# Chunk 0 of a Fourier mixing and gated feed-forward kernel: the E part added on TensorE, output-weight forms in pairs, weight pieces in another order

## The chip, the cores and the metric

The kernel runs on one core of one Trainium2 chip. The metric is the device time of one execution in microseconds (us). Engines are called TensorE (PE; PEld is its weight load), VectorE (DVE), ScalarE (ACT), GpSimd (POOL) and SyncE (SP, which here only issues DMA transfers).

## The reference

```python
x: (8, 3008, 256)                     # batch, sequence S, features D
X = fft(x, axis=1); X = fft(X, axis=2)
y = X.real.reshape(24064, 256)
gate = 1 / (1 + exp(-(y @ w_gate)))   # w_gate, w_val: (256, 1536)
val  = y @ w_val
out  = (gate * val) @ w_out           # w_out: (1536, 256)
```

All of it is float32 in the reference. The weights may arrive as 64-bit floats; the kernel then turns them into 32-bit ones itself.

## The kernel before, in words

The transform over the features is folded into the weights: `merge` (matmuls `ps`) multiplies pieces of `w_gate` and `w_val` by a 256-wide table `dt`, which gives G1 and G2. The transform over the sequence is done by matmuls with cosine and sine tables (`st`, matmuls `ev` and `od`), which give for each of the eight inputs a row set P (`pk`) and a row set Q (`qk`) over the frequencies. One extra row E (tile `ek`, for input 0) belongs to the middle feature. Frequency k and its mirror share the work: the pre-activation at one of them is G1·P + ge·E + G2·Q, at the other G1·P + ge·E − G2·Q.

**The main loop** runs over steps i: eight inputs, six chunks of 252 frequencies each, twelve steps for the twelve blocks of 128 hidden units. Chunk 0 of input 0 is steps 0 to 11. A step issues, in this order:

- `front_a(i)`: matmuls `pf<-pk,G` (G1·P), for gate and value, into a bank `PF[i]`. From step 12 on, ScalarE has put ge·E into the bank before (`seed`, L506).
- `part(i)`: `AP[i]` (tile `ae`), which keeps G1·P + ge·E before G2·Q comes in. Steps 0 to 11: two VectorE instructions L523. Later steps: one ScalarE instruction (L520) that doubles.
- `gate_a(i-1)` and `gate_b(i-1)`: the sigmoid on ScalarE (L539), the mirror's pre-activations z = 2·(G1·P + ge·E) − PF on VectorE (L541, or L544 where ScalarE doubled), gate times value (L556), the mirror's sigmoid on ScalarE (L557), its product on VectorE (L558), and the sums `sf` of H blocks on POOL (L562: seven in one step of three, six in the next).
- weights: what `pre`, `use` and `parts_` hold for the step (below).
- `back`: from step 5, ten matmuls `po` with a third of the 15 products of a group of three hidden blocks; they use `wf`, sums of quarter blocks of the output weights.
- `front_b(i)`: matmuls `pf<-qk,G` (G2·Q) into the same bank.

Before step 0 the row E is copied into the first 252 columns of row 0 of `qk` (L694), so that in chunk 0 these matmuls add ge·E to the bank themselves.

**Weights.** They come in 18 pieces (`jobs`: w is 0 gate, 1 value, 2 output; c counts 256 columns or rows). `weight_load` issues the DMA. `weight_parts` (two ScalarE instructions, L261 and L262) and `weight_join` (three on VectorE, L271, L272 and L274, then one on POOL, L276) turn a piece of 64-bit floats into 32-bit ones. `weight_use` runs `merge` on a gate or value piece (matmuls `ps`, then two ScalarE copies into G2 and G1, L297 and L298, and transfers `ge<-G` of row 0 of G2, L300), or, for an output piece, enters `forms(g)`: per group g of three blocks, 4 scaled copies on ScalarE (L315) and 11 sums or differences (L317), on POOL for g < 2 and on VectorE for g = 2, 3, in two parts of 6 and 5. One part is taken up per step. Pieces 0 to 8 are joined before step 0, piece 9 in step 0, pieces 10 to 17 in steps 1 to 8. Pieces from 10 on share three raw slots: the load of piece j+3 waits until POOL has joined piece j.

**Queues.** Every engine runs its instructions in the order in which the program issues them. The SP queue also waits, before each DMA, for the transfer eight lanes earlier. Before the loop, VectorE alternates between joining pieces and putting the sums of the transform in place (`then`, L420 and L423).

Of the kernel before, what the change touches and what calls it, by code (L numbers as in the profile page):

```python
# [48 lines left out]
NQ = 6  # L49
# [5 lines left out]
              (15, 4, 6, 1)),  # L55
          2: ((11, 8, 11, 0), (12, 8, 12, 0), (9, 5, 9, 0), (10, 10, 5, 0), (16, 2, 11, 0),
              (16, 9, 16, 0))}
W_SUMS = ((1, 5, 1), (3, 5, 1), (7, 2, 0), (6, 0, 0), (0, 7, 1), (4, 9, 0), (4, 8, 0), (3, 6, 1),
          (2, 3, 0), (2, 6, 1), (0, 1, 0))
W_COPIES = ((2, -1), (0, 1), (4, 1), (5, 1))  # L60

PRODUCTS = ((0, 12), (1, 11), (4, 9), (6, 4), (2, 13), (5, 5), (13, 0), (8, 6), (11, 2), (12, 8), (9, 3),
            (10, 10), (14, 1), (15, 7), (16, 14))
PLACE = (0, 1, 2, 5, 3, 4, 6, 7, 8, 9, 10, 11, 14, 13, 12)


# [11 lines left out]
def kernel(  # L78
# [108 lines left out]

    def load_table(t, nq):
        for q in range(0, NQ, nq):
            nc.sync.dma_start(out=ST[0][0:NP, t, q : q + nq], in_=stab[:, t, q : q + nq])  # L190

    def mirror_tables():
        return mirrored(tr, stab, NE)
# [7 lines left out]

    jobs = [(w, c - (w == 2)) for c in range(NPR + 1) for w in range(3)
            if (c if w == 2 else c < NPR)]
    RAW, WS = {}, {}
    shared = {}
    KEEP = 10
# [1 line left out]
    def weight_load(j):  # L210


        w, c = jobs[j]
        src = (moe_w_gate, moe_w_val, moe_w_out)[w]
        src = src[2 * c * P : 2 * (c + 1) * P, :] if w == 2 else src[:, c * WC : (c + 1) * WC]
        src = src.rearrange("(c p) f -> p c f", p=P)

        def some(n, pool, tag):

            if tag not in shared:  # L220
                shared[tag] = pool.tile([P, n * WC], F32, name=f"w{tag}", tag=tag)
            return shared[tag]

        def home(j):

            if j in (0, 1, 2, 3, 5):
                if j > 2:
                    ws = some(4, pqp, "qk")[:, (j // 5) * 2 * WC : (j // 5 + 1) * 2 * WC]
                    return sp.tile([P, 4 * WC], F32, name="raw", tag="sf"), ws
                t = hp.tile([P, 6 * WC], F32, name="raw", tag="h")  # L230
                return t[:, 0 : 4 * WC], t[:, 4 * WC :]
            if j in (4, 6, 9):
                t = wf[:, {4: 1, 6: 2, 9: 3}[j]].rearrange("p m n -> p (m n)")
                return t[:, 0 : 4 * WC], t[:, 4 * WC : 6 * WC]
            t = some(10, cp, "c")
            if j == 7:
                raw = pqp.tile([P, 4 * WC], F32, name="raw", tag="pk")
                return raw, t[:, 6 * WC : 8 * WC]
            return t[:, 0 : 4 * WC], t[:, 4 * WC : 6 * WC]

        if j < KEEP:
            raw, ws = home(j)
        else:
            both = some(24, xp, "x4").rearrange("p (i n) -> p i n", n=2 * WC)
            r, i = (j - KEEP) % 3 * 2, 6 + (j - KEEP) % 6
            raw, ws = both[:, r : r + 2].rearrange("p a n -> p (a n)"), both[:, i]
        raw = raw.bitcast(I32).rearrange("p (c f w) -> p c f w", c=2, w=2)
        ws = ws.rearrange("p (c f) -> p c f", c=2)
        WS[j] = ws
        if src.dtype == F32:  # L250
            nc.sync.dma_start(out=ws, in_=src)
        else:
            RAW[j] = raw
            nc.sync.dma_start(out=raw.rearrange("p c f w -> p c (f w)"), in_=src.bitcast(I32))
# [48 lines left out]
    def forms(g):  # L303

        w = [WO[f // 2].rearrange("p f (a h j) -> p f h a j", h=2, j=TB)[:, f % 2]
             for f in range(3 * g, 3 * g + 3)]
        f = wf[:, g].rearrange("p m (a j) -> p m a j", j=TB)
        engine = nc.gpsimd if g < 2 else nc.vector

        def block(i):  # L310
            return w[i // 2][:, i % 2] if i < 6 else f[:, i - 6]

        def some(lo, hi):
            for i, (a, sign) in enumerate(W_COPIES if lo == 0 else ()):
                nc.scalar.mul(f[:, len(W_SUMS) + i], block(a), float(sign))  # L315
            for i, (a, b, op) in list(enumerate(W_SUMS))[lo:hi]:
                engine.tensor_tensor(f[:, i], block(a), block(b), op=(ALU.subtract, ALU.add)[op])  # L317
        return [lambda lo=lo: some(lo, lo + 6) for lo in range(0, len(W_SUMS), 6)]


    W = {}
# [174 lines left out]
        nc.sync.dma_start(out=EK[i // NFT], in_=ed[b : b + 1, k0 : k0 + n].to_broadcast([P, n]))  # L496

    PF, AP, Z = {}, {}, {}

    def seed(i):  # L500


        _, _, n, f, _ = cut(i)
        PF[i] = bank("pf").rearrange("p (g n) -> p g n", g=2)[:, :, 0:n]
        for g in range(2 if i >= NFT else 0):
            nc.scalar.activation(PF[i][:, g], EK[i // NFT], AF.Copy, scale=ge[:, g, f : f + 1])  # L506

    def front_a(i):
        (pk, *_), ks, _, _, fs = cut(i)
        if i < NFT:  # L510
            seed(i)
        for g in range(2):
            mm(PF[i][:, g], G1[:, g, fs], pk[:, ks], i < NFT and g == 0, True)

    def part(i):

        pqe, ks, n, f, _ = cut(i)
        AP[i] = app.tile([P, 2, CH], F32, name="ae", tag="ae")[:, :, 0:n]
        if i >= NFT:
            nc.scalar.activation(AP[i], PF[i], AF.Copy, scale=2.0)  # L520
            return
        for g in range(2):
            nc.vector.scalar_tensor_tensor(out=AP[i][:, g], in0=pqe[2][:, ks],  # L523
                                           scalar=ge[:, g, f : f + 1], in1=PF[i][:, g],
                                           op0=ALU.mult, op1=ALU.add)
# [6 lines left out]
    def gate_a(i):  # L532

        n = cut(i)[2]
        p, fh = i // 3, i % 3
        z = Z[i] = zp.tile([P, 2, CH], F32, name="z", tag="z")[:, :, 0:n]
        if fh == 0:
            H[p] = hp.tile([P, 3, 2 * WC], F32, name="h", tag="h")[:, :, 0 : 2 * n]
        nc.scalar.activation(H[p][:, fh, 0:n], PF[i][:, 0], AF.Sigmoid)  # L539
        if i < NFT:  # L540
            nc.vector.scalar_tensor_tensor(out=z[:, :, ::-1], in0=AP.pop(i), scalar=2.0, in1=PF[i],  # L541
                                           op0=ALU.mult, op1=ALU.subtract)
        else:
            nc.vector.tensor_tensor(z[:, :, ::-1], AP.pop(i), PF[i], op=ALU.subtract)  # L544
# [113 lines left out]
    for j in range(2):  # L658
        weight_load(j)
    load_x(0)  # L660
    load_table(0, NQ // 2)
    for j in range(2, 6):
        weight_load(j)
    load_table(1, NQ)
    for j in range(6, KEEP):
        weight_load(j)

    def weight_round(*js):
        for j in js:
            weight_parts(j)  # L670
            weight_join(j)
# [5 lines left out]
    weight_use(0)  # L677
    weight_use(1)
    seq_start(0)
    other = {(0, 0): (4, None), (0, 1): (4, None), (0, 2): (0, 1), (1, 2): (2, 3)}  # L680
    cos = [seq_group(0, blk, what, other.get((blk, what))) for blk in range(2) for what in (0, 2)]
    for i, f in enumerate(fold_ops(0, NQ // 2)):
# [1 line left out]
        for sums, _, _ in cos:  # L684
            sums(*range(i * NQ // 2, (i + 1) * NQ // 2))
    sin = [seq_group(0, blk, 1, other.get((blk, 1))) for blk in range(2)]
    for sums, _, _ in sin:
        sums(*range(NQ))
    evacuate = [then for _, then, _ in cos + sin]
    for then, js in zip(evacuate, ((2, 3, 4), (5,), (), (), (6, 7), (8,))):  # L690
        weight_round(*js)
        then()()
    nc.scalar.dma_start(out=ed[0:1], in_=PQE[0][2][0:1])
    nc.vector.tensor_copy(PQE[0][1][0:1, 0:CH], PQE[0][2][0:1, 0:CH])  # L694
    for j in range(KEEP, KEEP + 3):
        weight_load(j)
    weight_use(2)
# [5 lines left out]
        side.setdefault(i, []).extend(fs)  # L703

    pre, use = {}, {}
    for j in range(9, len(jobs)):
        pre.setdefault(j - 9, []).append(lambda j=j: weight_round(j))
        if KEEP <= j < len(jobs) - 3:  # L710
            at(j - 9, lambda j=j: weight_load(j + 3))
    for j in range(3, len(jobs)):
        w, c = jobs[j]
        i = (0, 1, 4, 7, 9, 10)[c] if w == 2 else 2 * c - 3 + w
        use.setdefault(i, []).append(lambda j=j: weight_use(j))


    i0 = NFT
# [34 lines left out]

    for i in range(count):
        front_a(i)
        if i < NFT:
            part(i)
        if i:
            gate_a(i - 1)
        if i >= NFT:  # L760
            part(i)
        if i0 <= i + 1 < count:
            seed(i + 1)
        if i:
            gate_b(i - 1)
        todo = pre.pop(i, []) + use.pop(i, [])
        for f in [parts_.pop(0)] + todo if parts_ else todo + [lambda: parts_ and parts_.pop(0)()]:
            f()
        if i >= 5:
            back((i - 5) // 3, (i - 5) % 3)  # L770
        front_b(i)
        n = 3 if i >= count - 8 else 2 + i % 2
        for f in later[0:n]:
            f()
        del later[0:n]
        for f in side.pop(i, []):
            f()
# [55 lines left out]
```

## Time and profile before

| | |
|---|---|
| median of 3 runs | 1980.78 us (1980.3 to 1983.85) |
| profiled execution | 1978.69 us, span 1976.8 us |
| mean granted TensorE clock | 0.995 |
| TensorE, VectorE, ScalarE, POOL busy | 98%, 77%, 68%, 83% of the span |
| first `pk` matmul of step 0, 5, 8, 12 | 49.6, 69.3, 95.2, 111.9 us |

The profile is of one execution. Its page has the busy time of each engine, the span in 40 slices (a digit is tenths busy), the chain of work that ended last and the costliest groups of instructions. The trace answers finer questions: busy time by window, waits by releaser, and the instructions in order of time, where the bracket at the end of a line is how long the engine was idle before and what released it.

### The profile page before, as it was taken

To read this page: it belongs to the slowest core of one execution; us is meant where nothing else is said; L and a number is where in the kernel's file an instruction comes from. 1 tells how busy PE (TensorE), PEld (TensorE's weight loads), DVE (VectorE), ACT (ScalarE), POOL (GpSimd) and SP (SyncE) were. 2 spreads that over 40 slices of the span, in tenths; PEclk is the share of its full clock that TensorE was granted. 3 is DMA by queue.
4 is the path that set the end of the run, shared out by engine and by line. 5 is a ranking of instruction groups with operands and counts; after the bars stand their busy time and mean duration, and the time that the engine had idled before them with its cause. 6 is when DMAs were issued, how large, how long until landed. Compare 5 with 4: busy or idle time off the path is not lost.

```text
span 1976.8 us, 34387 instructions
## 1 busy us (share of the span) xinstructions
PE 1932.9 (98%) x11232; PEld 1788.1 (90%) x11232; DVE 1518.7 (77%) x3177; ACT 1337.7 (68%) x3103; POOL 1631.4 (83%) x2858
## 2 busy tenths in 40 slices
PE   6899999999999999999999999999999999999997
PEld 3689889998999899998999989999899999999997
DVE  7788778886787677786778867787678877777777
ACT  3467657775777667775777757777577766777774
POOL 3879888997889878997889868998688996777776
PEclk9999999999999999999999999999999999999999
DMA  7354413112012020212013021211210110011011
GB/s 267 88 132 93 137 31 110 47 26 77 14 47 58 14 78 14 66 39 77 15 25 80 15 78 23 47 49 22 77 20 14 20 21 14 14 19 22 14 19 27
DMA packets 171444, 101.41 MB, mean 51 GB/s; under 512 B 133890, under 2 KB 163204, under 8 KB 168588
## 3 DMA queue, kind: packets, MB, share of 16 engines
q1 hardware_dynamic: 169294, 98.64, 20.5%
q8 instruction: 90, 1.47, 0.3%
q10 hardware_dynamic: 1940, 0.56, 0.1%
q14 instruction: 88, 0.72, 0.1%
q0 software_dynamic: 32, 0.00, 0.0%
HBM read 74.45 MB, written 50.18 MB: 63 GB/s over the span
## 4 chain that ended last, share of the span: by engine, by line
PE 94%; DMA 2%; DVE 2%; ACT 1%; POOL 1%; issue 0%; ACTq 0%; DVEq 0%; SPq 0%; POOLq 0%
PE pf L129 48%; PE po L129 41%; PE ev L129 4%; DMA st<-in_stab_dram 1%; DMA ge<-G 1%; PE ps L129 1%; PE od L129 1%; DVE wf L317 0%; DMA raw<-in_moe_w_val_dram 0%; DVE ae L523 0%; DVE z L541 0%; POOL sf L562 0%; DVE h L558 0%; POOL wf L317 0%; DVE c L609 0%
## 5 line engine op out<-in xcount | busy, mean ns | idle before, releaser
L562 POOL TENSOR_TENSOR sf<-h 128x168 f32<-128x168 f32 (+1 forms) x960 | 549.3, 591 | 222.0 <-DVE h L558 221.9
L562 POOL TENSOR_TENSOR sf<-h,sf 128x168 f32<-128x168 f32 (+1 forms) x1152 | 657.6, 591 | 58.7 <-DVE h L558 58.7
L129 PE MATMUL pf<-qk,G 128*128 128x252 f32 (+1 forms) x2304 | 582.6, 376 | 3.2 <-DVE ae L523 1.9
L129 PE MATMUL pf<-pk,G 128*128 128x252 f32 (+1 forms) x2304 | 582.9, 376 | 0.0
L558 DVE TENSOR_TENSOR h<-z 128x252 f32<-128x252 f32 (+1 forms) x576 | 301.3, 523 | 350.7 <-ACT z L557 350.1
L506 ACT ACTIVATE pf<-ek,ge 128x252 f32<-128x252 f32 (+1 forms) x1128 | 531.5, 471 | 18.5
L129 PE MATMUL po<-sf,wf 128*128 128x168 f32 (+1 forms) x3072 | 530.1, 306 | 0.0
L520 ACT ACTIVATE ae<-pf 128x504 f32<-128x504 f32 (+1 forms) x564 | 332.6, 590 | 234.4 <-PE pf L129 233.6
L609 DVE TENSOR_TENSOR c<-c 128x168 f32<-128x168 f32 (+1 forms) x949 | 484.8, 542 | 5.5 <-ACT c L586 0.3
L129 PEld LDWEIGHTS pf<-pk,G 128*128 128x128 f32 x2304 | 436.3, 190 | 53.0 <-issue 2.3
L129 PEld LDWEIGHTS po<-sf,wf 128*128 128x128 f32 x3072 | 473.0, 190 | 8.5
L129 PE MATMUL po<-h,wf 128*128 128x168 f32 (+1 forms) x2688 | 475.9, 305 | 2.1 <-ACT a L473 1.6
L129 PEld LDWEIGHTS po<-h,wf 128*128 128x128 f32 x2688 | 427.4, 190 | 19.2 <-ACT a L473 2.0
L129 PEld LDWEIGHTS pf<-qk,G 128*128 128x128 f32 x2304 | 409.9, 190 | 30.0 <-DVE ae L523 2.9
L544 DVE TENSOR_TENSOR z<-ae,pf 128x504 f32<-128x504 f32 (+1 forms) x564 | 374.3, 664 | 17.6 <-ACT h L539 17.1
L539 ACT ACTIVATE h<-pf 128x252 f32<-128x252 f32 (+1 forms) x576 | 218.5, 379 | 164.4 <-PE pf L129 152.7
L557 ACT ACTIVATE z<-z 128x252 f32<-128x252 f32 (+1 forms) x576 | 231.1, 401 | 91.0 <-DVE z L544 59.5
L556 DVE TENSOR_TENSOR h<-h,pf 128x252 f32<-128x252 f32 (+1 forms) x576 | 232.2, 403 | 0.0
L562 POOL TENSOR_TENSOR sf<-sf 128x168 f32<-128x168 f32 (+1 forms) x192 | 111.4, 580 | 15.0
L129 PE MATMUL ev<-st,x 63*128 63x376 f32 (+4 forms) x372 | 97.6, 414 | 9.7 <-DVE x L340 8.0
L562 POOL TENSOR_TENSOR sf<-sf,h 128x168 f32<-128x168 f32 (+1 forms) x192 | 106.7, 556 | 0.0
L129 PEld LDWEIGHTS ev<-st,x 63*128 63x128 f32 (+1 forms) x372 | 66.4, 187 | 37.4 <-DVE x L340 8.4
(115 smaller groups left out, 870.0 us busy)
## 6 DMA issues: line engine op xcount, KB each, us to landing
x<-xr SPq DMA_DIRECT2D x14, 1536.0 KB
out_dram<-os SPq DMA_DIRECT2D x380, 56.0 KB
xr<-in_xf_dram SPq DMA_DIRECT2D x14, 768.0 KB
xr<-in_xf_dram SPq DMA_DIRECT2D x35, 256.0 KB
ek<-ed SPq DMA_DIRECT2D x39, 126.0 KB
out_dram<-os SPq DMA_DIRECT2D x288, 7.0 KB
x<-in_xf_dram SPq DMA_DIRECT2D x2, 1512.0 KB
tr<-in_stab_dram SPq DMA_DIRECT2D x2, 1129.5 KB
```

The costliest lines, as they stand in the source:

```text
L129: nc.tensor.matmul(o, l, r, start=start, stop=stop, skip_group_check=True)
L506: nc.scalar.activation(PF[i][:, g], EK[i // NFT], AF.Copy, scale=ge[:, g, f : f + 1])
L520: nc.scalar.activation(AP[i], PF[i], AF.Copy, scale=2.0)
L539: nc.scalar.activation(H[p][:, fh, 0:n], PF[i][:, 0], AF.Sigmoid)
L544: nc.vector.tensor_tensor(z[:, :, ::-1], AP.pop(i), PF[i], op=ALU.subtract)
L556: nc.vector.tensor_tensor(h[:, fh, 0:n], h[:, fh, 0:n], PF.pop(i)[:, 1], op=ALU.mult)
L557: nc.scalar.activation(z[:, 0], z[:, 0], AF.Sigmoid)
L558: nc.vector.tensor_tensor(h[:, fh, n:], z[:, 0], z[:, 1], op=ALU.mult)
L562: nc.gpsimd.tensor_tensor(block(p, dst), block(p, a), block(p, b), op=(ALU.subtract, ALU.add)[op])
L609: engine.tensor_tensor(t[:, dst * R : (dst + 1) * R], *v, op=(ALU.subtract, ALU.add)[op])
```

## The change

It has four parts, all in what comes before step 12.

1. *E part.* For steps 0 to 4 (`N1 = 5`), `front_a` adds two matmuls that multiply G2 by a block `e0` of 128 x 252, zero but for row 0, which holds E (cleared on POOL, one row copied on VectorE before step 0). `part` then doubles the bank on ScalarE, as in later chunks, and z takes one VectorE subtraction. Steps 5 to 11 stay as they were. The copy of E into row 0 of `qk` goes from before step 0 to the end of step 4.
2. *Forms of output weights.* The 11 sums are 6 entries, five of them of two blocks at a time (128 x 256). Where two blocks don't lie at one stride in one tile, the entry falls apart into single ones: groups 0 and 2 have 6 instructions, groups 1 and 3 have 9. They come in three parts of two entries, and group 1 goes from POOL to VectorE; only group 0 stays on POOL. The order of the blocks in `wf` changes, and `PRODUCTS` with it.
3. *Pieces.* `jobs` is written out: gate 4 comes ahead of output 2, gate and value 5 ahead of output 3. Each piece's ScalarE half is issued a step earlier than its VectorE and POOL half, so piece 9's before step 0; `weight_use` of the output pieces 0 and 1 is in step 0.
4. *Before the loop.* The second half of the tables (sine) is loaded in two transfers, after pieces 4 and 6, and its matmuls go half by half through both sums. The joins of pieces 2 to 8 are spread evenly over the six evacuations.

```diff
-W_SUMS = ((1, 5, 1), (3, 5, 1), (7, 2, 0), (6, 0, 0), (0, 7, 1), (4, 9, 0), (4, 8, 0), (3, 6, 1),
-          (2, 3, 0), (2, 6, 1), (0, 1, 0))
+W_SUMS = (((1, 3), (5,), 1, 6), ((6, 7), (0, 2), 0, 8), ((4,), (8, 9), 0, 10), ((6,), (2, 3), 1, 12),
+          ((0, 2), (1, 3), 0, 14), ((0,), (7,), 1, 16))
-    jobs = [(w, c - (w == 2)) for c in range(NPR + 1) for w in range(3)
-            if (c if w == 2 else c < NPR)]
+    jobs = [(0, 0), (1, 0), (0, 1), (1, 1), (2, 0), (0, 2), (1, 2), (2, 1), (0, 3), (1, 3), (0, 4), (2, 2),
+            (1, 4), (0, 5), (1, 5), (2, 3), (2, 4), (2, 5)]
...
-        engine = nc.gpsimd if g < 2 else nc.vector
+        engine = nc.vector if g else nc.gpsimd
...
+        def blocks(ij, n):
+            i, j = ij[0], ij[-1]
+            if i == j:
+                return one(i).unsqueeze(1).to_broadcast([P, n, 4, TB])
+            if i >= 6:
+                return f[:, i - 6 : j - 5]
+            if i // 2 == j // 2:
+                return w[i // 2]
+            lo = 3 * g + i // 2
+            if lo % 2 == 0 and j // 2 == i // 2 + 1:
+                return WO[lo // 2].rearrange("p f (a h j) -> p h f a j", h=2, j=TB)[:, i % 2]
+            return None
+        def sums(lo, hi):
+            for x, y, op, to in W_SUMS[lo:hi]:
+                n = max(len(x), len(y))
+                a, b = blocks(x, n), blocks(y, n)
+                op = (ALU.subtract, ALU.add)[op]
+                if a is not None and b is not None:
+                    engine.tensor_tensor(f[:, to - 6 : to - 6 + n], a, b, op=op)
+                else:
+                    for i in range(n):
+                        engine.tensor_tensor(f[:, to - 6 + i], one(x[i % len(x)]), one(y[i % len(y)]), op=op)
+        return [lambda: (copies(), sums(0, 2)), lambda: sums(2, 4), lambda: sums(4, 6)]
...
+    N1 = 5
...
+        for g in range(2 if i < N1 else 0):
+            mm(PF[i][:, g], G2[:, g, fs], shared["qk"][:, 4 * WC : 4 * WC + CH], False, True)
...
-        if i >= NFT:
+        if not N1 <= i < NFT:
             nc.scalar.activation(AP[i], PF[i], AF.Copy, scale=2.0)
             return
...
-    load_table(1, NQ)
-    for j in range(6, KEEP):
+    sines = load_table(1, NQ // 2)
+    next(sines)
+    for j in range(5, 7):
+        weight_load(j)
+    next(sines)
+    for j in range(7, KEEP):
         weight_load(j)
...
+    e0 = shared["qk"][:, 4 * WC : 4 * WC + CH]
+    nc.gpsimd.memset(e0, 0.0)
...
-    for sums, _, _ in sin:
-        sums(*range(NQ))
+    for i in range(2):
+        for sums, _, _ in sin:
+            sums(*range(i * NQ // 2, (i + 1) * NQ // 2))
...
-    for then, js in zip(evacuate, ((2, 3, 4), (5,), (), (), (6, 7), (8,))):
+    for then, js in zip(evacuate, ((2, 3), (4,), (5,), (6,), (7,), (8,))):
...
-    nc.vector.tensor_copy(PQE[0][1][0:1, 0:CH], PQE[0][2][0:1, 0:CH])
+    nc.vector.tensor_copy(e0[0:1], PQE[0][2][0:1, 0:CH])
+    weight_parts(9)
...
-    for j in range(9, len(jobs)):
-        pre.setdefault(j - 9, []).append(lambda j=j: weight_round(j))
+    for j, i in enumerate((0, 1, 2, 3, 4, 5, 6, 7, 9), 9):
+        if i:
+            pre.setdefault(i - 1, []).append(lambda j=j: weight_parts(j))
+        pre.setdefault(i, []).insert(0, lambda j=j: weight_join(j))
...
-    for j in range(3, len(jobs)):
-        w, c = jobs[j]
-        i = (0, 1, 4, 7, 9, 10)[c] if w == 2 else 2 * c - 3 + w
+    for j, i in enumerate((0, 0, 1, 2, 0, 3, 4, 5, 4, 6, 7, 8, 8, 8, 11), 3):
         use.setdefault(i, []).append(lambda j=j: weight_use(j))
+    at(N1 - 1, lambda: nc.vector.tensor_copy(PQE[0][1][0:1, 0:CH], PQE[0][2][0:1, 0:CH]))
```

In the changed file the lines stand 1 to 38 further down: L277 is POOL's part of a join, L301 the transfer of `ge`, L551 the old L523, L548 the doubling, L334 and L337 the forms in pairs and singly, L586 the old L558.

More of the change, by code (lines that the diff above doesn't have):

```diff
@@ L57 @@
               (16, 9, 16, 0))}
-W_SUMS = ((1, 5, 1), (3, 5, 1), (7, 2, 0), (6, 0, 0), (0, 7, 1), (4, 9, 0), (4, 8, 0), (3, 6, 1),
-          (2, 3, 0), (2, 6, 1), (0, 1, 0))
+W_SUMS = (((1, 3), (5,), 1, 6), ((6, 7), (0, 2), 0, 8), ((4,), (8, 9), 0, 10), ((6,), (2, 3), 1, 12),
+          ((0, 2), (1, 3), 0, 14), ((0,), (7,), 1, 16))
 W_COPIES = ((2, -1), (0, 1), (4, 1), (5, 1))
-PRODUCTS = ((0, 12), (1, 11), (4, 9), (6, 4), (2, 13), (5, 5), (13, 0), (8, 6), (11, 2), (12, 8), (9, 3),
-            (10, 10), (14, 1), (15, 7), (16, 14))
+PRODUCTS = ((0, 12), (1, 11), (4, 6), (6, 10), (2, 13), (5, 4), (13, 0),
+            (8, 5), (11, 3), (12, 9), (9, 2), (10, 8), (14, 1), (15, 7), (16, 14))
 PLACE = (0, 1, 2, 5, 3, 4, 6, 7, 8, 9, 10, 11, 14, 13, 12)
@@ L189, in load_table @@
         for q in range(0, NQ, nq):
-            nc.sync.dma_start(out=ST[0][0:NP, t, q : q + nq], in_=stab[:, t, q : q + nq])
+            yield nc.sync.dma_start(out=ST[0][0:NP, t, q : q + nq], in_=stab[:, t, q : q + nq])
     def mirror_tables():
@@ L200, in table_again @@
             nc.sync.dma_start(out=ST[0][:, t, N3:, NE:], in_=tr[:, t, N3:, NE:])
-    jobs = [(w, c - (w == 2)) for c in range(NPR + 1) for w in range(3)
-            if (c if w == 2 else c < NPR)]
+    assert NPR == 6
+    jobs = [(0, 0), (1, 0), (0, 1), (1, 1), (2, 0), (0, 2), (1, 2), (2, 1), (0, 3), (1, 3), (0, 4), (2, 2),
+            (1, 4), (0, 5), (1, 5), (2, 3), (2, 4), (2, 5)]
     RAW, WS = {}, {}
@@ L227, in home @@
                 if j > 2:
-                    ws = some(4, pqp, "qk")[:, (j // 5) * 2 * WC : (j // 5 + 1) * 2 * WC]
+                    ws = some(5, pqp, "qk")[:, (j // 5) * 2 * WC : (j // 5 + 1) * 2 * WC]
                     return sp.tile([P, 4 * WC], F32, name="raw", tag="sf"), ws
@@ L307, in forms, with one, copies @@
         f = wf[:, g].rearrange("p m (a j) -> p m a j", j=TB)
-        engine = nc.gpsimd if g < 2 else nc.vector
-        def block(i):
+        engine = nc.vector if g else nc.gpsimd
+        def one(i):
             return w[i // 2][:, i % 2] if i < 6 else f[:, i - 6]
[L313 to L318, printed above, removed]
+        def blocks(ij, n):
[20 more added lines that the diff above has]
+                        engine.tensor_tensor(f[:, to - 6 + i], one(x[i % len(x)]), one(y[i % len(y)]), op=op)
+        def copies():
+            for i, (a, sign) in enumerate(W_COPIES):
+                nc.scalar.mul(f[:, 11 + i], one(a), float(sign))
+        return [lambda: (copies(), sums(0, 2)), lambda: sums(2, 4), lambda: sums(4, 6)]
     W = {}
@@ L539, in gate_a @@
         nc.scalar.activation(H[p][:, fh, 0:n], PF[i][:, 0], AF.Sigmoid)
-        if i < NFT:
+        if N1 <= i < NFT:
             nc.vector.scalar_tensor_tensor(out=z[:, :, ::-1], in0=AP.pop(i), scalar=2.0, in1=PF[i],
@@ L660 @@
     load_x(0)
-    load_table(0, NQ // 2)
-    for j in range(2, 6):
+    for _ in load_table(0, NQ // 2):
+        pass
+    for j in range(2, 5):
         weight_load(j)
-    load_table(1, NQ)
-    for j in range(6, KEEP):
+    sines = load_table(1, NQ // 2)
[4 more added lines that the diff above has]
+    for j in range(7, KEEP):
         weight_load(j)
@@ L707 @@
     pre, use = {}, {}
-    for j in range(9, len(jobs)):
-        pre.setdefault(j - 9, []).append(lambda j=j: weight_round(j))
+    for j, i in enumerate((0, 1, 2, 3, 4, 5, 6, 7, 9), 9):
+        if i:
+            pre.setdefault(i - 1, []).append(lambda j=j: weight_parts(j))
+        pre.setdefault(i, []).insert(0, lambda j=j: weight_join(j))
         if KEEP <= j < len(jobs) - 3:
-            at(j - 9, lambda j=j: weight_load(j + 3))
-    for j in range(3, len(jobs)):
-        w, c = jobs[j]
-        i = (0, 1, 4, 7, 9, 10)[c] if w == 2 else 2 * c - 3 + w
+            at(i, lambda j=j: weight_load(j + 3))
+    for j, i in enumerate((0, 0, 1, 2, 0, 3, 4, 5, 4, 6, 7, 8, 8, 8, 11), 3):
         use.setdefault(i, []).append(lambda j=j: weight_use(j))
+    at(N1 - 1, lambda: nc.vector.tensor_copy(PQE[0][1][0:1, 0:CH], PQE[0][2][0:1, 0:CH]))
     i0 = NFT
@@ L755 @@
         front_a(i)
-        if i < NFT:
+        if N1 <= i < NFT:
             part(i)
@@ L759 @@
             gate_a(i - 1)
-        if i >= NFT:
+        if not N1 <= i < NFT:
             part(i)
```

## The prediction

> **What bounds the kernel now.** I read the busy rows first, then the chain of waits, then one stretch at a time. Over the whole span TensorE is the bound, but not in the first 120 us.
>
> ```profile
> PE 1932.9 (98%) x11232; PEld 1788.1 (90%) x11232; DVE 1518.7 (77%) x3177; ACT 1337.7 (68%) x3103; POOL 1631.4 (83%) x2858
> PE   6899999999999999999999999999999999999997
> ```
>
> Only 43.9 us of 1976.8 are free of matmuls, and the low digits stand in the first three slices. The table of windows, cut at the starts of chunk 0's steps 5, 6, 7, 8 and 9, and one steady stretch:
>
> ```profile
> 69.30:75.50 6.20, 5.01 (x26) 4.29 (x26) 5.40 (x9) 3.21 (x12) 6.12 (x10) 1.00 0.34 85
> 75.50:82.30 6.80, 5.61 (x28) 4.41 (x27) 4.83 (x7) 2.43 (x7) 6.72 (x10) 1.00 0.52 149
> 82.30:95.20 12.90, 6.90 (x26) 5.66 (x26) 8.19 (x12) 4.26 (x11) 12.82 (x20) 0.74 0.22 55
> 95.20:100.00 4.80, 4.80 (x27) 4.42 (x26) 3.16 (x7) 2.41 (x6) 2.66 (x5) 1.00 0.01 0
> 121.80:160.00 38.20, 38.20 (x221) 35.96 (x220) 28.71 (x64) 28.35 (x66) 30.82 (x55) 1.00 0.69 127
> ```
>
> Columns: length, then busy of PE, PEld, DVE, ACT, POOL, then granted clock. In steps 5 to 7 POOL is full (6.12 of 6.20, 6.72 of 6.80, 12.82 of 12.90) and TensorE is not; after 121.8 TensorE is full. The chain and the timeline name the worst place:
>
> ```profile
> 71.61 3.86 DMA wx<-in_moe_w_gate_dram
> 85.89 2.24 POOL wf L317 x5
> 88.13 1.25 POOL wx L276
> 89.43 3.78 PE ps L129 x8
> ...
> 88.09 1.28 POOL L276 TENSOR_TENSOR wx<-wx 128x512 int32<-128x512 int32 x1
> 89.43 3.78 PE L129 MATMUL ps<-wx,dt 128*128 128x256 f32 x8 [6.00 <-POOL wx L276]
> ```
>
> TensorE waits 6.00 us in step 7 for the last operation of a piece of weights (L276), which stands in POOL's queue behind the forms of output weights (L317); its eight matmuls then take 3.78 us where the others take 1.89, at a granted clock of 0.74.
>
> From the starts of the `pk` matmuls the steps began at 49.6, 53.0, 56.4, 60.4, 64.5, 69.3, 75.5, 82.3, 95.2, 100.1, 103.2, 108.0, 111.9, 115.1, 118.4, and step 15 at 121.8. TensorE's own work is 1.70 (eight `pf`) + 1.73 (`ps`) = 3.43 in steps 0 to 4, 4.86 with `po` (1.43) in 5 to 8, 3.13 from 9: 17.2 + 19.4 + 18.8 = 55.4 of the 72.2 us to step 15. So 16.8 us are to be had, no more.
>
> **The change part by part.**
>
> *E part on TensorE.* Adds two matmuls to each of steps 0 to 4. The two `pk` matmuls are x4 records in 0.85 us: +0.85 a step, +4.25, on TensorE's queue and with no cover where TensorE is the bound. It removes two L523 from VectorE in each (0.86, so -4.3), and gives ScalarE the doubling (0.59, the L520 row). ScalarE now has, per step, 0.38 + 0.59 + 0.41 + 1.34 (a piece) + 0.62 (two copies of G) = 3.3 of 4.28: covered. But L557 now stands behind the doubling, which waits for the new matmuls: VectorE's L558 comes no earlier than 1.7 + 0.6 + 0.4 = 2.7 us into a step, and VectorE idles some 1.5 us in each of steps 1 to 3.
>
> *Row of E.* POOL clears the block at about 10 us, where it waits for x until 16.75: nothing (0.3 if not covered). The 1-row copy (0.74) now holds the `pf<-wqk` matmuls of step 0 on TensorE; it is last in VectorE's queue before the loop (49.91 before). The second copy, after step 4, waits for TensorE's `qk` matmuls of that step, with VectorE's step 5 queued behind; VectorE gets there later than they do.
>
> *Sine table in halves.* Before, sine matmuls began at 40.39, 1.67 after the others, for the table landed 15.52 us after its issue at 24.74. The SP queue's waits come from DMA lanes, so the first half takes the issue slot of 21.39 and the second that of 26.18. Half the bytes, issued earlier, land by about 34; the second by 38 to 42, needed at 42.5. So the sine matmuls begin at 38.7 and end near 46.4 (48.2 before). Piece 5 moves behind the half (issue 24.74 for 21.39, under 36 by 1.14 MB at the 307 GB/s of that stretch, from a start no later than 32.2), VectorE wants it at 37. VectorE, busy 19.54 of 20 us there, saves only its 1.30 us wait for piece 6, less about 0.4: its end is 49.1 for 49.95. Step 0: `pk` at 48.1, then the matmuls of E wait for the copy until 49.8; step 1 starts at 53.2, against 53.0. The earlier sine is thus eaten by the copy.
>
> *Forms.* Group 0 stays on POOL, a step earlier: 5 of 128x256 and one of 128x128. No such row exists on POOL: 128x128 takes 0.45, 128x512 1.29, so between 0.45 and 1.29; by the line through both 0.75. 5 x 0.75 + 0.45 = 4.2 for 5.75 (59.88 to 63.39, 67.88 to 70.13). Two thirds fall into POOL's 3.98 us idle before 58.63. Group 1 leaves POOL: -5.45 (78.14 to 81.36, 85.86 to 88.09). For VectorE it is 9 instructions and not 6, as an odd group's blocks lie in two tiles: the pairs fall apart there, in group 3 too. On VectorE the L317 row has 22 in 9.6 us of pitch, 0.44 each: 9 x 0.44 = +4.0; group 2 falls from 11 to 6 (-1.9), group 3 to 9 (-0.9).
>
> The row says that a form on VectorE takes 0.28 us alone and 0.62 beside POOL. The Trainium skill (SBUF — State Buffer, section "SBUF: two separate sides") says that a VectorE instruction with two SBUF inputs and a GpSimd one lock each other out for a whole instruction, which speaks against moving forms: then 9 x 0.62 = 5.6 on VectorE, and POOL gets back 5.45 less 9 x 0.28. Gain by the row 7.0, by the rule about 5.5. I take 0.44, measured beside a POOL 66% busy, as here.
>
> *Pieces.* ScalarE's half is done a step ahead, so VectorE no longer waits for it (1.9 us in four waits of L271). But it now stands ahead of the copies of G, and `ps` of the next step waits for these. The load of the piece that ScalarE takes in step 4 is issued only when POOL has finished the second piece of the loop.
>
> *SP's queue.* The loads of pieces 10 to 12 wait for the last sine matmul, so they go out at 46.4 for 48.30; ScalarE wants piece 10 at 51.4, and before it landed 3.9 after its issue: no wait. The columns `ge` (L301) stand behind the loads as before, where VectorE waited 1.10 for one at 80.8; with L523 gone from steps 0 to 4 the first is wanted in step 5, after it was loaded: nothing, and 1.1 if a load holds them.
>
> The queues together, by those durations (a piece on VectorE 1.6 to 2.5, 1.3 on POOL; seven `sf` 4.5, six 3.9):
> - Steps 1 to 5 start at 53.2, 57.5, 61.8, 66.1, 70.4 (TensorE-bound, 4.28 each). POOL: second piece done at 67.8 (71.6 before), load landed at 71.7, ScalarE's copies of G at 73.3, so `ps` of step 5 waits from 71.3 to 73.4.
> - VectorE ends step 4's forms and copy at 73.9, and its L523 (0.86), z (0.67), h (0.83), forms (1.0, 1.3) and a piece (2.5) then set the pace: steps 6 to 9 start at 77.3, 82.2, 87.8, 92.7. No 6 us wait of TensorE is left, for the piece of step 7 is joined at 74, and no slow clock.
> - Steps 10 to 12 at 96.1, 101.7, 105.0 (front_b waits for L523 behind forms 2 and the last piece); 13 to 15 at 108.3, 111.5, 114.8.
>
> Step 15 at 114.8 for 121.8: -7.0. From there TensorE is full, and what follows hangs on step numbers, so it all moves along. Profiled execution: 1978.69 (span 1976.8 + 1.9), so 1971.7. The median of the three runs is 2.1 above that execution: 1973.7, I say 1974.
>
> **The rivals.**
> - *TensorE-bound throughout.* If VectorE's instructions run at their lone durations (a piece 1.54, a form 0.28), only TensorE's work counts: from 48.1, 0.85 for the copy, 21.4 + 19.4 + 18.8: step 15 at 108.5, -13.3: 1967.5. For: VectorE sheds 2.5 net. Against: L271 to L274 took 2.3 to 3.1 in steps 4 to 8.
> - *ScalarE's early half holds TensorE.* If POOL's second piece is done at 71.6 as before, its load lands at 75.5, the copies of G come at 77.4 and step 5's `ps` 4 us later than in my sum: gain 3, 1978. For: POOL was the queue to slip here. Against: forms 0 start 5 us earlier.
> - *VectorE the bound, and slower.* From step 4 it has 4.0 us of forms more, and TensorE waits for L523 in each step. Its 55.5 us of work from 50 to step 15 need to grow by 13% (7.0) for no gain; at 20% the time is +4.1: 1985. For: a form's 0.28 to 0.62. Against: I took the crowded durations already.
> - *Half of the pairing doesn't happen* (groups 1 and 3): in the sum; if group 0 fell apart too, 11 forms on POOL, +1.5.
>
> **How the numbers follow.** A measurement of this kernel can tell about 0.2% (4 us) from no change. My sum, gain 4 to 10: 0.56. TensorE-bound, over 10: 0.18. Early half, within 4 either way: 0.19. VectorE slower: 0.07. So faster 0.74, same 0.19, slower 0.07. Range 1967 (the TensorE-bound end) to 1980, leaving out the last case and the weak end of the third.
>
> **What would show it.** Right: `pf<-wqk` matmuls x20 with 0.85 us a step; no wait of `ps` for L277 over 1 us; step 5 starting later than 69.3 by about 1, step 8 near 88, step 15 near 115; DVE the releaser of `qk` matmuls in steps 5 to 10; clock 1.00 from 70 to 95. Wrong: step 15 past 118 with POOL full before it; sine matmuls still at 40; ScalarE waiting over 3 us for a load ahead of a copy of G.

## The result, and the profile after

The changed kernel takes 1973.84 us (median of 6 runs, 1972.83 to 1975.21), the kernel before 1980.38 us (median of 6). The ratio is 0.9965, with a 95% interval from 0.9952 to 0.9978: 4.4 to 9.5 us faster. The profiled execution took 1973.76 us with a span of 1972.0, against 1978.69 and 1976.8 before: 4.8 us less span. The forecast was 1974 with a range of 1967 to 1980.

The page of the changed kernel, the busy row of TensorE and its row of slices:

```profile
PE 1935.8 (98%) x11252; PEld 1792.4 (91%) x11252; DVE 1511.7 (77%) x3170; ACT 1339.5 (68%) x3108; POOL 1625.0 (82%) x2843
...
PE   6999999999999999999999999999999999999997
```

TensorE has 20 records more and is busy 2.9 us longer; its second slice went from 8 tenths to 9. The windows from the starts of steps 5, 6, 7, 8, 9 and 11, and a steady stretch after step 15 (length; busy of PE, PEld, DVE, ACT, POOL; granted clock; DMA share; GB/s):

```profile
71.20:78.10 6.90, 5.49 (x28) 4.41 (x27) 6.83 (x12) 3.11 (x10) 4.54 (x6) 1.00 0.44 115
78.10:83.90 5.80, 5.10 (x27) 4.29 (x26) 5.43 (x12) 2.57 (x8) 4.90 (x6) 1.00 0.23 75
83.90:89.50 5.60, 5.10 (x27) 4.39 (x27) 5.38 (x12) 2.44 (x7) 4.99 (x7) 1.00 0.36 94
89.50:94.40 4.90, 4.90 (x28) 4.49 (x27) 4.68 (x10) 2.15 (x6) 2.87 (x5) 1.00 0.03 0
94.40:103.00 8.60, 6.60 (x38) 5.98 (x37) 8.00 (x16) 2.86 (x11) 7.58 (x12) 1.00 0.38 112
103.00:107.70 4.70, 4.70 (x20) 4.38 (x18) 4.39 (x11) 2.57 (x9) 2.33 (x5) 0.64 0.63 205
...
117.40:156.00 38.60, 38.60 (x223) 36.30 (x223) 28.10 (x64) 27.78 (x65) 30.97 (x54) 1.00 0.71 126
```

In steps 5 to 7 it is now VectorE that is full (6.83 of 6.90, 5.43 of 5.80, 5.38 of 5.60), POOL no longer; in step 8 it is TensorE (4.90 of 4.90). Step 7, which took 12.90 us, takes 5.6. TensorE's waits that are left in chunk 0 (total, times, longest):

```profile
PE ps L129 <- ACT G L299: 2.0, 2, 1.3
PE pf L129 <- DVE ae L551: 2.0, 1, 2.0
...
PE pf L129 <- DVE wqk L731: 0.8, 1, 0.8
```

Four places in the timeline:

```profile
44.67 0.43 DVE L272 TENSOR_SCALAR wc<-wc 128x512 f32<-128x512 f32 x1 [2.18 <-ACT wc L262]
...
50.81 1.12 PE L129 MATMUL pf<-wqk,G 128*128 128x252 f32 x4 [0.78 <-DVE wqk L731]
...
73.81 1.96 PE L129 MATMUL ps<-wx,dt 128*128 128x256 f32 x8 [1.35 <-ACT G L299]
...
102.15 1.12 PE L129 MATMUL pf<-qk,G 128*128 128x252 f32 x4 [2.00 <-DVE ae L551]
```

The 6.00 us wait of `ps` for POOL's L276 is gone. What is left is the copy of E ahead of step 0, ScalarE's copies of G in steps 5 and 6, 0.5 us for POOL's sums in step 7, and VectorE's L551 in step 10. In step 5 the copies of G stand behind a piece whose load ScalarE waits 1.62 us for. In step 6 they stand behind L585, which waits for VectorE, so that VectorE holds TensorE over ScalarE:

```profile
77.83 0.41 ACT L585 ACTIVATE z<-z 128x252 f32<-128x252 f32 x1 [3.09 <-DVE z L572]
79.54 0.38 ACT L299 COPY G<-ps 128x256 f32<-128x256 f32 x1
80.06 1.97 PE L129 MATMUL ps<-wx,dt 128*128 128x256 f32 x8 [0.70 <-ACT G L299]
```

The starts of the `pk` matmuls, one profiled execution of each kernel, are the measure of the experiments too. They show where a time comes from better than the medians, whose intervals are some 5 us wide: steps 1 to 11 take 48.8 us in each of the changed kernel, e3 and e7, which issue the same there. Two things still differ from execution to execution: the loads, which move steps 0 and 1, and TensorE's clock, worth 1.4 us in step 11 (last section). (The prediction counted from the weight loads of these matmuls, 0.2 us earlier.) The last column leaves out the start of step 0.

| kernel | step 0 | 1 | 5 | 8 | 11 | 15 | 0 to 15 |
|---|---|---|---|---|---|---|---|
| before | 49.8 | 53.2 | 69.4 | 95.4 | 108.2 | 121.9 | 72.1 |
| changed | 49.0 | 54.3 | 71.5 | 89.7 | 103.1 | 117.6 | 68.6 |
| e1 | 49.0 | 52.8 | 70.5 | 89.3 | 102.7 | 115.5 | 66.5 |
| e2 | 49.0 | 53.6 | 70.7 | 87.5 | 102.0 | 116.5 | 67.5 |
| e3 | 52.1 | 56.6 | 73.7 | 92.0 | 105.3 | 118.2 | 66.0 |
| e4 | 50.9 | 55.4 | 72.5 | 97.8 | 110.5 | 124.2 | 73.3 |
| e5 | 50.2 | 53.6 | 71.3 | 90.1 | 103.0 | 116.0 | 65.8 |
| e6 | 49.7 | 55.1 | 72.2 | 90.8 | 104.8 | 117.7 | 68.0 |
| e7 | 48.5 | 52.7 | 69.8 | 88.1 | 101.5 | 116.0 | 67.5 |
| e8 | 48.2 | 53.0 | 70.2 | 88.4 | 101.0 | 116.6 | 68.4 |
| e9 | 56.2 | 60.5 | 77.6 | 94.2 | 108.9 | 121.8 | 65.6 |
| e10 | 48.8 | 52.2 | 70.1 | 87.1 | 103.2 | 116.1 | 67.3 |
| e11 | 50.7 | 54.1 | 71.8 | 90.4 | 104.5 | 117.4 | 66.7 |
| e12 | 48.6 | 52.9 | 70.0 | 86.7 | 101.2 | 115.8 | 67.2 |

Step 15 comes 4.3 us earlier in the changed kernel (121.9 less 117.6), which is nearly all of the span's 4.8.

### The profile page after: what moved, and what is told of

Read it like the earlier page. It is cut to its first block, busy times and chain, and to the rows that moved or that the text cites. A ratio compares the mean times of both kernels' runs of the same rounds, so it can differ in the third digit from the quotient of the medians.

```text
span 1972.0 us, 34403 instructions
## 1 busy us (share of the span) xinstructions
PE 1935.8 (98%) x11252; PEld 1792.4 (91%) x11252; DVE 1511.7 (77%) x3170; ACT 1339.5 (68%) x3108; POOL 1625.0 (82%) x2843
## 4 chain that ended last, share of the span: by engine, by line
PE 95%; DMA 2%; DVE 2%; ACT 1%; issue 0%; POOL 0%; SPq 0%; ACTq 0%; DVEq 0%; POOLq 0%
PE pf L129 49%; PE po L129 41%; PE ev L129 4%; DMA st<-in_stab_dram 1%; PE ps L129 1%; DMA ge<-G 1%; PE od L129 0%; DMA raw<-in_moe_w_val_dram 0%; DMA xr<-in_xf_dram 0%; DVE c L637 0%; DVE ae L551 0%; DVE wf L337 0%; DVE wx L273 0%; ACT z L585 0%; DVE wx L275 0%
## 5 line engine op out<-in xcount | busy, mean ns | idle before, releaser
L590 POOL TENSOR_TENSOR sf<-h,sf 128x168 f32<-128x168 f32 (+1 forms) x1152 | 657.2, 590 | 60.5 <-DVE h L586 60.5
L586 DVE TENSOR_TENSOR h<-z 128x252 f32<-128x252 f32 (+1 forms) x576 | 299.1, 519 | 356.9 <-ACT z L585 356.6
L548 ACT ACTIVATE ae<-pf 128x504 f32<-128x504 f32 (+1 forms) x569 | 335.0, 589 | 245.6 <-PE pf L129 245.5
L585 ACT ACTIVATE z<-z 128x252 f32<-128x252 f32 (+1 forms) x576 | 231.1, 401 | 80.3 <-DVE z L572 60.1
```

What stands on the lines that cost most here:

```text
L585: nc.scalar.activation(z[:, 0], z[:, 0], AF.Sigmoid)
L586: nc.vector.tensor_tensor(h[:, fh, n:], z[:, 0], z[:, 1], op=ALU.mult)
L590: nc.gpsimd.tensor_tensor(block(p, dst), block(p, a), block(p, b), op=(ALU.subtract, ALU.add)[op])
```

## The experiments

The theory after the result: the gain is that of POOL's queue, which got rid of the forms, and VectorE's queue is the bound that took its place, in most of steps 5 to 10. The rivals: the E part pays by what it takes off VectorE; the earlier pieces or the split sine table pay.

**The forms alone (e5).** The kernel before with part 2:

```diff
-W_SUMS = ((1, 5, 1), ...            # 11 sums
+W_SUMS = (((1, 3), (5,), 1, 6), ... # 6 entries, as in the change; PRODUCTS and forms() too
-        i = (0, 1, 4, 7, 9, 10)[c] if w == 2 else 2 * c - 3 + w
+        i = (0, 0, 4, 7, 8, 11)[c] if w == 2 else 2 * c - 3 + w
```

> The kernel before with part 2 alone: forms in pairs where they pair, in three parts, group 1 on VectorE, taken up at steps 0, 4, 8 and 11 as in the changed kernel; pieces, E part and loads as before. Theory (POOL's queue was the bound of steps 3 to 8, so this part carries the gain): TensorE's wait of 6 us for L276 in step 7 falls below 2, step 8 starts at 88 to 91 (95.4 before), step 15 at 115.5 to 118 (121.9), time 4 to 6 us under before. Rival (the gain needs the earlier pieces, part 3): the wait stays above 4 us, step 15 at 119.5 or later, time under 2.5 us from before.

1975.75 us, ratio 0.9971 (0.9960 to 0.9982). Step 8 at 90.1, step 15 at 116.0, 5.9 us earlier than before and 1.6 earlier than with the whole change (1.3 of which is the clock, below). All waits of TensorE in the stretch from 40 to 130:

```profile
PE ps L129 <- ACT G L298: 4.1, 7, 0.7
PE pf L129 <- DVE ae L546: 2.5, 3, 1.2
PE ev L129 <- DMA st<-in_stab_dram: 1.1, 1, 1.1
```

No wait for L276 is left. Part 2 alone does what the change does, as far as the ratios can tell.

**The E part alone (e4).** The kernel before with part 1 (the block `e0`, N1 = 5, the doubling on ScalarE, the second copy after step 4), nothing else.

> The kernel before with part 1 alone: E on TensorE and the doubling on ScalarE in steps 0 to 4, all else as before. Theory (POOL's queue paces steps 3 to 8 of the kernel before): the 4.25 us more of TensorE lie in its waits; step 5 starts 1 us later than 69.3, step 8 within 1.5 us of 95.2, step 15 within 1.5 us of 121.8, time within 2 us of before. Rival 1 (TensorE's work adds): step 15 at 126, time +4. Rival 2 (VectorE was the bound and sheds 4.3): step 15 at 118, time -4.

1981.88 us, ratio 1.0006 (0.9997 to 1.0014). Step 5 is 3.1 us later than before, step 8 2.3, step 15 2.3, more than the theory's 1.5; but 1.2 us of that stand already at step 0, for in this execution the sine matmuls got their table 1.16 later (at 41.55 for 40.39). From step 0, step 15 is 1.2 later: some 3 of the 4.25 us are hidden, as the theory had it. The interval of the time, 0.6 us less to 2.8 more, leaves out both rivals (4 more, 4 less). The wait that they lie in is there in full:

```profile
PE ps L129 <- POOL wx L276: 6.5, 2, 6.1
```

What is not hidden is step 0 (4.4 us for 3.4), before POOL's queue is full.

**The change without the E part (e1).**

```diff
-    N1 = 5
+    N1 = 0
-    nc.vector.tensor_copy(e0[0:1], PQE[0][2][0:1, 0:CH])
+    nc.vector.tensor_copy(PQE[0][1][0:1, 0:CH], PQE[0][2][0:1, 0:CH])
...                                  # the clearing of e0 and the second copy go too
```

> The changed kernel with the E part as before: TensorE adds no E (N1 = 0), VectorE does L523's work in all of steps 0 to 11, E is copied into row 0 of qk ahead of step 0. Theory (VectorE sets the pace from step 4 on): TensorE is 4.25 us shorter in steps 0 to 4, VectorE 4.3 us longer, less some 3 us that it idled there; step 5 starts 0 to 3 us earlier than the changed kernel's 71.2, but step 15 lies within 2 us of its 117.4 and the time within 2 us of 1973.8. Rival (TensorE sets the pace in steps 0 to 4 and the E part costs its 4.25 us): step 15 at 113, time 1969.5.

1973.12 us, ratio 0.9968 (0.9952 to 0.9983): no difference from the changed kernel that the runs can tell. Step 5 is 1.0 earlier, step 11 0.4 earlier; step 15 is 2.1 earlier, just outside the theory's 2, but 1.4 of that is step 11 itself, which takes 3.4 us here and 4.8 in the changed kernel at a lowered clock (below). VectorE's waits from 46 to 72, first of the changed kernel, then of e1:

```profile
DVE z L572 <- ACT h L567: 3.2, 1, 3.2
DVE h L586 <- ACT z L585: 3.1, 4, 1.3
...
DVE ae L551 <- PE pf L129: 0.9, 1, 0.9
DVE h L586 <- ACT z L585: 0.6, 4, 0.2
```

The 4.3 us that the E part takes off VectorE are idled: 6.3 us of waits for 1.5. It brings nothing that these runs can tell.

**Group 1 on POOL (e2, e11).** In the changed kernel (e2), and in e5 (e11):

```diff
-        engine = nc.vector if g else nc.gpsimd
+        engine = nc.gpsimd if g < 2 else nc.vector
```

> The changed kernel with the forms of group 1 on POOL again, in pairs where they pair. Theory (VectorE paces steps 5 to 10, POOL has 5.7 us of gaps from 73 to 92): VectorE sheds the 9 instructions (3.6 us), POOL takes them into its gaps at some 0.5 us each; step 9 starts 1 to 3 us earlier than 94.4, step 15 at 115 to 117, time 1971 to 1974. Rival (POOL's queue was the bound of before and taking group 1 off it is what the gain is made of): TensorE waits for L277 again in steps 6 to 8, step 15 at 120 to 122, time 1977 to 1979.

e2: 1972.86 us, ratio 0.9960 (0.9945 to 0.9975). Step 9 at 92.4 for 94.6, step 15 at 116.5 for 117.6, with the same low clock in step 11: inside the theory's ranges. But 0.8 us of this stand at step 1, up to which the two kernels are the same. From there e2 takes 1.4 us less in steps 5 to 7, where VectorE is relieved, and 1.0 more in steps 9 and 10, where VectorE waits 1.19 us for POOL's L277 behind the forms and TensorE then 2.6 for L551:

```profile
92.75 0.75 DVE L334 TENSOR_TENSOR wf<-wx 128x256 f32<-128x256 f32 x1 [1.19 <-POOL wx L277]
```

> e5 (the kernel before with the forms part alone) with group 1 on POOL: what stays is the pairing and the earlier start of groups 0. Theory (POOL's queue, 5.5 us earlier by pairing and an earlier start, with 5 us of gaps from 73 to 92, has room for group 1): TensorE's wait for L276 stays below 2 us, step 15 at 114.5 to 117, as e5's 116.0 or better. Rival (taking group 1 off POOL is what e5 gains by): the wait comes back above 3 us, step 15 at 119 or later.

e11: 1975.12 us, ratio 0.9969 (0.9956 to 0.9982), step 15 at 117.4, 1.0 later than e5 when counted from step 0 (66.7 for 65.8), and

```profile
PE ps L129 <- POOL wx L276: 2.5, 1, 2.5
```

That lies between the two. Of the 6.0 us wait for POOL, pairing and the earlier start of group 0 take some 3.5 (no run tells them apart), group 1's move the rest; by the ratios e11 and e5 are alike. With the pieces in the new order and their ScalarE half a step ahead (e2), the move is not needed and costs 0.4 us from step 1 on.

**The sine table whole (e3).** Part 4 undone: one transfer after piece 5, its matmuls sum by sum, the joins as before.

> The changed kernel with part 4 taken back: the sine table in one transfer after piece 5, its matmuls sum by sum, joins of pieces 2 to 8 ahead of the evacuations 1, 2, 5 and 6. Theory (VectorE's queue and not the table sets the start of step 0): sine matmuls end 2 us later, but the copy of E still ends at about 50.7 and step 1 starts at 54 as now; step 15 within 1 us, time within 1.5 us of 1973.8. Rival (the early half brings TensorE forward): step 1 at 55 to 56, time 1 to 2 us longer.

1976.16 us, ratio 0.9977 (0.9970 to 0.9985), 2.3 more than the changed kernel, with intervals that overlap a little. In its profile, sine matmuls wait again:

```profile
PE ev L129 <- DMA st<-in_stab_dram: 1.9, 1, 1.9
```

Step 1 comes at 56.6, 2.2 later, and steps 1 to 11 take the same 48.8. But its loads came later throughout (the table was issued at 26.65, in the kernel before at 24.74; the first cosine matmul came at 22.29, in the changed kernel at 21.39), so of the 2.2 at least 0.9 is that execution's, which took 2.0 us more than the median of its kernel. The theory of no effect does not hold by the medians (15 runs against 6), and the rival's 1 to 2 us come near; how much the split itself brings stays open.

**ScalarE's half in the step of the join (e6).** `weight_round(j)` in place of the two halves, the order of the pieces kept.

> The changed kernel with ScalarE's half of pieces 9 to 17 in the step of their join, not a step ahead (the order of the pieces stays). Theory: VectorE waits for ScalarE again, 0.2 to 0.6 us in each of eight steps, but in step 4 ScalarE no longer waits 1.62 us for a load ahead of the copies of G, and the 1.35 us wait of ps in step 5 goes; step 15 within 1.5 us of 117.6, time within 1.5 us of 1973.8. Rival (the early half is what frees VectorE): step 15 at 120 or later, time +2.5. Rival 2 (the early half holds TensorE): step 15 at 115.5, time -2.

1974.57 us, ratio 0.9966 (0.9956 to 0.9975). Steps 1 to 11 take 49.8 for 48.8: the early half is worth about 1.0 us; step 15 is the same, as the clock did not drop here. The waits of VectorE for ScalarE that the theory had in eight steps did not come, but for one of 2.4 us, for piece 9. As expected, TensorE's longest wait for the copies of G fell from 1.35 to 0.7, and it waits twice for L551, 4.0 us in sum.

**The copy of E earlier (e7).**

```diff
+        if js == (6,):
+            nc.vector.tensor_copy(e0[0:1], PQE[0][2][0:1, 0:CH])
-    nc.vector.tensor_copy(e0[0:1], PQE[0][2][0:1, 0:CH])
```

> The changed kernel with the one-row copy of E into its block right after the fourth evacuation, where VectorE idles 2.18 us for a piece, and not after the sixth. Theory (VectorE's last instruction before the loop sets the start of step 0's E matmuls): TensorE's wait of 0.78 us for L731 goes, step 1 starts 0.7 to 0.9 us earlier than 54.3, VectorE is 0.66 us ahead from there, and step 11 starts about 0.7 us earlier than 103.1; time -0.7 (and 1.4 us more or less, by whether TensorE's clock drops in step 11). Rival (VectorE's waits further on eat it): step 11 at 103.1.

1973.58 us, ratio 0.9966 (0.9953 to 0.9979). The wait for L731 is gone, and steps 1, 5 and 11 each start 1.6 earlier. About half of that can be laid to the loads of the execution: VectorE, which waits 2.18 us for piece 7 in the changed kernel's profile, waits 0.21 for it in e2's, whose code is the same up to there. Against e2, step 1 comes 0.8 earlier (52.7 for 53.6), which is what was expected; it is too little for the medians.

**Group 2 on POOL (e8).** `engine = nc.vector if g % 2 else nc.gpsimd`.

> The changed kernel with the forms of group 2 (six instructions, five of them pairs) on POOL too. Theory (VectorE is the bound of steps 9 and 10, where TensorE waits 2.00 us for L551): VectorE sheds 3 us there, POOL has gaps of some 4 us from 90 to 107 for 4.1 us; the wait of 2.00 falls below 0.8, step 11 starts 1 to 2 us earlier than 103.1, and with no drop of the clock step 15 at 114.5 to 116.5, time 1971 to 1973. Rival (POOL slips and po of step 11 waits for its forms): step 11 as now, step 12 later by 1 us or more, time +1.

1975.99 us, ratio 0.9973 (0.9962 to 0.9984). Each was half right:

```profile
PE po L129 <- POOL wf L334: 2.2, 2, 2.0
...
PE pf L129 <- DVE ae L551: 1.2, 1, 1.2
```

The wait for VectorE in step 10 falls from 2.0 to 1.2, not below 0.8, and counted from step 0 step 11 starts 1.3 earlier; but in step 11 TensorE waits 2.0 for POOL's forms, and by step 12 the gain is down to 0.3 us (58.6 us from step 0 for 58.9), with no low clock here and one in the changed kernel.

**Together (e9, e10, e12).** e9 is e7 and e2 with the last piece a step earlier, e10 is e1 and e2 with that:

```diff
-    for j, i in enumerate((0, 1, 2, 3, 4, 5, 6, 7, 9), 9):
+    for j, i in enumerate((0, 1, 2, 3, 4, 5, 6, 7, 8), 9):
```

> The changed kernel with three edits together: the copy of E early (as in e7), forms of group 1 on POOL (as in e2), and the VectorE and POOL half of the last piece in step 8 for step 9. Theory (VectorE is the bound of steps 5 to 10): step 5 at 69.2 (e2's 70.7 less e7's gain), step 8 at 86, and the wait for L551 of 2.6 us in e2's step 10 falls below 1.5 as the piece is done a step earlier; step 11 at 98 to 100, step 15 at 111 to 113.5 (111 is near the 110 of TensorE's own work), time 1968 to 1971. Rival (the wait only moves to step 9, and the gain is e7's alone): step 11 at 101, step 15 at 114 to 116, time 1971.5 to 1973.

> The changed kernel without the E part (as in e1), group 1's forms on POOL and the last piece a step earlier. Theory (the E part on TensorE is worth nothing by itself, for what VectorE sheds it idles away behind ScalarE): step 5 at 69.5 to 70.5, step 15 within 1 us of e9's. Rival (with VectorE relieved of group 1, the E part pays): step 15 2 us or more after e9's.

e9: 1973.83 us, ratio 0.9962 (0.9948 to 0.9976); e10: 1973.92 us, ratio 0.9969 (0.9955 to 0.9983). Step 8 lasts 8.2 us in e9 and 9.9 in e10, in the changed kernel 4.9. ScalarE's half of the last piece, now in step 7, has to wait for POOL's forms of group 1, whose weights lie in the same place, with the copies of G behind it. From the waits of e9, a line of those of all engines from 76 to 106 us:

```profile
ACT wx L262 <- POOL wf L337: 4.1, 1, 4.1
```

and one of TensorE's, from 40 to 130:

```profile
PE ps L129 <- ACT G L299: 4.8, 3, 3.1
```

The theory and the rival of e9 both miss this. From step 0 to 15 e9 takes 65.6 and e10 67.3, between e10's theory (within 1 us) and its rival (2 or more); the difference is step 8, where e10's clock fell (0.91 over 80 to 100 us): E on TensorE is worth nothing measurable here either. (e9's profiled execution began step 0 7 us late, by its loads.)

> The changed kernel with the copy of E early (e7) and group 1's forms on POOL (e2), the last piece where it was (step 9). Theory (the two gains add: e7 starts step 5 1.7 us earlier than the changed kernel, e2 shortens steps 5 to 9 by 1.4 us; e9 and e10 lost theirs to ScalarE's 4.1 us wait for POOL's forms ahead of the last piece, which is gone here): 66.5 to 67 us from step 0 to step 15 with one drop of the clock, 65 without (68.6 in the changed kernel), TensorE waiting once, 2 to 2.7 us for L551 in step 10; time 1971 to 1972.5. Rival (what is gained ahead of step 10 waits there for the last piece): step 0 to 15 within 1 us of 68.6, time within 1 us of 1973.8.

e12: 1971.21 us (5 runs, 1970.0 to 1971.99), ratio 0.9954 (0.9940 to 0.9967), the fastest of all. 67.2 us from step 0 to 15 with the low clock in step 11, for 68.6, a little over what was expected. Besides the wait for L551 in step 10 (2.60), the one for the copies of G in step 5 (1.35) is still there:

```profile
PE pf L129 <- DVE ae L551: 3.0, 2, 2.6
PE ps L129 <- ACT G L299: 1.6, 2, 1.4
```

Its interval and that of the changed kernel overlap; the medians are 2.6 us apart.

## Why the prediction was right, point by point

- *POOL's queue as the bound of steps 5 to 7, and the forms as what frees it*: right, and e5 shows it: 5.9 us at step 15 from part 2 alone. The sum counted on group 1 leaving POOL as well; e11 shows that pairing and the earlier start of group 0 do most of it. (The prediction calls the first three slices low; they read 6, 8 and 9.)
- *VectorE as the next bound*: right in the main. The steps were put at 70.4 (5), 77.3, 82.2, 87.8, 92.7 (9), 96.1, 101.7 (11); they came at 71.2, 78.1, 83.9, 89.5, 94.4, 97.5, 103.0 by the weight loads. The copies of G held TensorE in step 5 (expected 2.1, measured 1.35), L551 in step 10. But the sign named, VectorE as the releaser of the `qk` matmuls in steps 5 to 10, is there in step 10 alone: in step 6 VectorE holds TensorE over ScalarE, in step 8 TensorE is full. VectorE's work from 50 us to step 15, put at 55.5 us, came to 57.0.
- *Forms.* A pair on POOL was put at 0.75; it took 0.73, which is what the line through the two rows gives. Group 1 on VectorE was put at 9 x 0.44 = 4.0; its three parts took 1.9, 1.0 and 1.0. That the sum was met is in part luck, for three of the nine are pairs. The other estimate, 5.6, took all nine to run beside POOL. POOL was idle during the first three (0.28 each); the fourth began 0.07 us after POOL's L277 and ended 0.15 after it. This fits a lock for a whole instruction; what was too high is how often it would strike.

```profile
73.91 0.28 DVE L337 TENSOR_TENSOR wf<-wc,wx 128x128 f32<-128x128 f32 x1
74.45 1.29 POOL L277 TENSOR_TENSOR wx<-wx 128x512 int32<-128x512 int32 x1 [1.02 <-ACT G L299]
74.52 1.37 DVE L337 TENSOR_TENSOR wf<-wf,wx 128x128 f32<-128x128 f32 x1
```

- *The E part*: +4.25 on TensorE and -4.3 on VectorE were both in the sum, and that VectorE would idle behind the doubling. Right in kind; with and without it (e1) the times can't be told apart.
- *Sine table and copy of E*: the step that was off by 0.9 us. "The earlier sine is eaten by the copy" held, but the second half was needed at 42.4 and the matmul that waited for it began at 42.92, and piece 7 behind it so late that VectorE waited 2.18 us, where the sum had it wait less than before. Step 1 came at 54.1 and not at 53.2. These are the loads of one execution: in e2 and e8, the same up to there, VectorE waited 0.21 and 0.62 us for piece 7, and step 1 came at 53.4 and 52.8 by the weight loads.
- *Steps 11 to 15*: the sum had 13.1 us, measured 14.4. Missing in it is TensorE's clock, 1.4 us in step 11.

So step 15 came 2.6 us later than the sum had it: 0.9 at step 1, 0.4 up to step 11, 1.3 from there. 0.4 came back after step 15, and the span's gain was 4.8 for 7.0. Between the medians it was 6.5, for the profiled execution of before was 1.7 under the median of its six runs, that of after 0.1. So the forecast of 1974 was met so closely by luck: the sum put the profiled execution at 1971.7 and it took 1973.76, 2.1 more; and the 2.1 that the forecast added for the distance to the median was 0.1.

Of the rivals, ScalarE's early half did hold TensorE, for 1.35 us; TensorE was not the bound throughout; VectorE's work was 3% more than in the sum, not 13.

## What to carry to other kernels

When an in-order queue is full, look at what stands in it that others do not wait for yet: here fewer and larger instructions on that queue, started a step earlier (e11), brought the gain of the whole change to within what the runs can tell, and moving work off VectorE to two others brought nothing, because VectorE then waited. Work issued a step ahead takes its waits along: each such move must be followed to what stands behind it on its queue, as the last piece in e9 shows. And when the gain is a few us, read it from the starts of the steps of one profile, with the start of the first step and the clock as a check.

## What the runs showed of the hardware that was not expected

TensorE's clock dropped to half after a gap of only 2.00 us. In the changed kernel (length; busy of PE, PEld, DVE, ACT, POOL; granted clock):

```profile
100.08:103.49 3.41, 1.41 (x7) 1.23 (x7) 3.22 (x7) 0.60 (x2) 3.33 (x5) 1.00 0.49 162
103.49:106.91 3.42, 3.42 (x12) 3.21 (x12) 3.27 (x8) 1.80 (x7) 1.23 (x3) 0.50 0.55 174
106.91:110.32 3.41, 3.41 (x21) 3.23 (x21) 2.88 (x7) 2.15 (x7) 2.68 (x5) 1.00 0.54 190
```

In e1, after a gap of the same length at the same place, it stayed at full, and in e9 even after a longer one:

```profile
101.71 1.12 PE L129 MATMUL pf<-qk,G 128*128 128x252 f32 x4 [2.00 <-DVE ae L551]
...
98.38 1.97 PE L129 MATMUL ps<-wx,dt 128*128 128x256 f32 x8 [3.12 <-ACT G L299]
```

The traces show what decides it. Each low stretch between the loads and the end is 3.41 us long, or twice that (6.83 in the kernel before, 86.48 to 93.30); within one trace the edges of all of them lie on a grid of 3.41 us, and the grid lies elsewhere in each execution. In the changed kernel the gap falls into one cell of it (a stretch between two edges), the first row above: 2.00 of 3.41 us idle. In e1 and e9 an edge of the grid (counted on from a low stretch at 18.60 in e1, at 49.03 in e9) cuts the gap in two:

```profile
97.11:100.52 3.41, 2.61 (x16) 2.24 (x14) 3.31 (x6) 0.38 (x1) 2.82 (x5) 1.00 0.74 229
100.52:103.94 3.42, 2.23 (x11) 2.05 (x12) 3.27 (x8) 1.45 (x4) 2.92 (x4) 1.00 0.26 91
...
93.40:96.81 3.41, 1.86 (x10) 1.33 (x8) 2.63 (x5) 0.32 (x1) 3.33 (x6) 1.00 0.39 127
96.81:100.23 3.42, 1.85 (x9) 1.67 (x10) 1.52 (x4) 2.12 (x6) 3.42 (x5) 1.00 0.04 0
```

So counted over all fourteen traces from 45 us to near the end, each cell with 2.00 us idle or more (in the kernel before, the changed one, e2, e4, e7, e9, e10 and e12) was followed by a low one, and none with less than 1.85; of the five between, two were (e3 and e4, at 209 and 215 us). The Trainium skill (TensorE: Matmul & The Clock Gate, section "Part 1: The HAM clock gate (the "warmup" mystery)") puts the drop at an idle window of about 3.4 us that runs freely; the traces agree on the length and on the window not being tied to the work, but 2.00 us idle within one were enough here. The price was 1.4 us: step 11 took 4.8 us with the drop and 3.4 without. A forecast to the microsecond can't know this term ahead: where the grid falls differs from execution to execution.
